# Masked global rows transposed on TensorE instead of by DMA, in a fused attention and SwiGLU kernel

## The chip, the cores and the metric

The kernel runs on one core of a Trainium2 chip. The metric is device time in microseconds for one execution, as the median of several runs. TensorE (PE) multiplies, VectorE (DVE), ScalarE (ACT) and GpSimd (POOL) do elementwise work, SyncE (SP) only issues DMAs here. Each engine works through its own queue in order.

## The reference

Eight batches of eight heads, 576 positions, head size 64. A query attends to the keys within 32 positions of it and to 8 global positions; the 8 global positions themselves attend to every key. The attention output then goes through a SwiGLU block of width 512 and inner width 1536.

```python
scores = scale * np.matmul(q, k.transpose(0, 1, 3, 2))
mask = np.abs(pos[:, None] - pos[None, :]) <= 32
mask = mask | is_global[:, None] | is_global[None, :]
attn = softmax(np.where(mask, scores, -1e9))        # over keys
x = np.matmul(attn, v).transpose(0, 2, 1, 3).reshape(4608, 512)
g = x @ w_gate
out = (g * sigmoid(g) * (x @ w_val)) @ w_out
```

Input and output are float32; the kernel multiplies in bfloat16.

## The kernel before

**FFN.** The 4608 tokens are worked in 9 chunks of 512. A chunk has 16 units (function `ffn`): 12 gate units (`gate`, L806: four matmuls for `pg` and four for `pv`, then ScalarE's tanh at L837 and VectorE's two products at L839 and L843) and 4 output units (`outp`, L867: twelve matmuls, ScalarE's copy at L872, SyncE's store at L874). The units use four one-bank PSUM buffers (tag "f"), so a unit can start when the unit two before it has been read out.

**Attention.** It is cut into steps, and each step is put by hand into the gap behind a unit of the FFN. Batch b's steps lie in chunk b-1 (gap 0 of batch b is behind unit 16(b-1); a gap of -1 is behind the last unit of the chunk before). Batch 0 runs ahead of everything, and batch 1 in chunk 0. For batch b from 2 on:

- `cast_qk` (L110, POOL) casts q and k to bfloat16 copies in DRAM; `transpose_qk` (L117, L121, SyncE) brings them back transposed as kT and qT. `load_v` (L103, POOL) loads the values va, and `load_vb` (L130, L131, SyncE) makes a copy vb that is shifted by 64 positions.
- `gather` (L252, POOL, once per two batches) fetches the rows of k and q at the global positions, kg and qg, 128 rows each, which hold 8 heads and 8 positions of both batches. `gather_mask` (L262, POOL) multiplies them with a 0/1 mask that puts each row into its place for one batch. The result is kqm: part 0 from k, part 1 from q.
- `step_GT` transposes both parts to gT. Before the change, batches 0 and 1 do it on TensorE and copy from PSUM on VectorE (L424, L429), and batches 2 to 7 by one DMA transpose on SyncE (L418).
- `step_S2` (L457) multiplies gT's part 1 with kT: the scores of the global queries against all keys. ScalarE exponentiates (L464) and VectorE masks with a table (L469), giving p2.
- `step_SG` (L435) multiplies part 0 with qT: the scores of all queries against the global keys. Exponential at L442, mask at L447, giving pg.
- `step_P2T` transposes p2 to p2t: on TensorE, with a ScalarE copy (L482, L486), for batches below XP, otherwise by a DMA on SyncE (L478).
- `step_AV2` (L492) uses p2t and va; `step_S` (L523) makes the band scores; `step_AV` (L601, L610) and `step_AV8` (L629, L637) multiply with the values and are normalised on VectorE (L577 to L583); `step_X` and `step_X8` transpose the result into xT, from batch 2 on by DMAs on SyncE (L648, L689).

A chunk c needs xT for tokens 512c to 512c+511, so chunk 2 needs the first three xT tiles of batch 2.

**Masks and parity.** In the rows of a gather, the two batches of a pair alternate in groups of 16. After the transposition the columns of an odd batch therefore stand in the other half of each group of 32 than those of an even one. Before the change each parity has its own tables: pg is masked with `mg` or, in odd batches, `mt`; p2 with `mg2` or `mg2o`. `mg2o` is made by POOL in `tables_odd` (L349 to L354) out of `cnt`, a ScalarE copy (L345) of a PSUM tile, and is put ahead of batch 1's loads in `loads_b`.

**Order.** Nothing is reordered: each engine's queue has the order in which the program calls the steps. PSUM has a pool "m" with one two-bank buffer, which step_SG, step_AV and the TensorE transposes share, and "sc" with one, for step_S2, step_S and step_AV8. The gaps of batches from 3 on, before:

```python
-1: [L(step_GT)],
1: [vb],
2: [L(step_S2), L(step_SG)] + ([L(step_P2T)] if b >= XP else []),
4: [L(step_S, 0)] + ([] if b >= XP else [L(step_P2T)]),
7: [L(step_S, 1), L(step_AV2)],
```

Of the kernel before, what the change touches and what calls it, by code (L numbers as in the profile page):

```python
# [9 lines left out]
FP32 = mybir.dt.float32  # L10
BF16 = mybir.dt.bfloat16
# [3 lines left out]
ALU = mybir.AluOpType  # L15
AX = mybir.AxisListType

P = 128
# [8 lines left out]
def kernel(  # L27
# [11 lines left out]
    nc = tc.nc  # L39

    B, H, S, D = q.shape
# [3 lines left out]
    WIN = 32  # L45
# [4 lines left out]
    HP = H // 2  # L50
    LP = 96
    LJ = S // LP
    KC = S + 2 * WIN
    XQ = 2
    XG = 2
    XB = 2
    XP = 3
    W = D + 2

    assert (B, H, S, D, NG, DM, DF) == (8, 8, 576, 64, 8, 512, 1536)  # L60
# [2 lines left out]
    const = ctx.enter_context(tc.tile_pool(name="const", bufs=1))  # L63
# [4 lines left out]
    gw = ctx.enter_context(tc.tile_pool(name="gw", bufs=2))  # L68
# [89 lines left out]
    iq = const.tile([P, KC], FP32)  # L158
# [12 lines left out]
    mt = const.tile([P, KC], BF16)  # L171
# [6 lines left out]
    def va_clear(i, eng=nc.vector):  # L178
# [8 lines left out]
        out=oh16.rearrange("p h a r -> p (h a r)"),  # L187
        in_=ident.rearrange("p (a g) -> p a g", g=NG), axis=AX.X, op=ALU.add,
# [3 lines left out]
        out=p8, in_=ident.rearrange("p (a g) -> p g a", g=NG), axis=AX.X, op=ALU.add  # L192
# [9 lines left out]
        out=mka, in_=oh16.rearrange("p h a r -> p a r h"), axis=AX.X, op=ALU.add  # L202
    )
    asel = const.tile([P, 2], FP32)
# [4 lines left out]
        out=hb, in0=bc(asel[:, 1:2], [[-1, 2]]), scalar1=float(H * S), scalar2=None, op0=ALU.mult  # L209
    )  # L210
    nc.vector.tensor_tensor(
        out=bofs_f, in0=bofs_f, in1=bc(hb, [[1, 2], [0, B // 2]]), op=ALU.add
# [4 lines left out]
        out=tmp8h, in0=dmask.rearrange("p h r -> p (h r)"), in1=i8_f, op=ALU.mult  # L217
# [4 lines left out]
        out=gidx_f, in_=gidx_i64.bitcast(I32).rearrange("p (a b) -> p a b", b=2)[:, :, 0]  # L222
# [8 lines left out]
        out=hrow, in0=hrow, scalar1=float(S), scalar2=gcol, op0=ALU.mult, op1=ALU.add  # L231
# [3 lines left out]
    thr = const.tile([P, 2], FP32)  # L235
    nc.vector.tensor_scalar(
        out=thr, in0=asel, scalar1=R2 + 0.25, scalar2=-0.25, op0=ALU.mult, op1=ALU.add
# [2 lines left out]
    nc.vector.tensor_scalar(  # L240
        out=sgn, in0=asel, scalar1=2.0, scalar2=-1.0, op0=ALU.mult, op1=ALU.add
    )
    thi = const.tile([P, 2], FP32)
    nc.vector.tensor_scalar(
        out=thi, in0=asel, scalar1=1e6, scalar2=0.5, op0=ALU.mult, op1=ALU.add
    )

    def gather(i):
# [35 lines left out]
    load_wgv(0)  # L284
    load_wgv(1)
    def loads_b():
        tables_odd()
        kT_clear(1, nc.gpsimd)
        va_clear(1, nc.gpsimd)
        gather_mask(1, *g0)  # L290
        loaded[1] = new_qk()
        load_qk_part(1, loaded[1], 0)
        load_qk_part(1, loaded[1], 1)
        load_wgv(2)
        load_v(1)
        for i in range(4):
            nc.gpsimd.dma_start(
                out=wo_sb[:, 3 * i : 3 * i + 3, :],
                in_=moe_w_out[3 * P * i : 3 * P * (i + 1), :].rearrange(
                    "(fc p) m -> p fc m", p=P  # L300
                ),
            )


    mg = const.tile([P, KC], BF16)
    mg2 = const.tile([P, KC], BF16)
    mg2o = const.tile([P, KC], BF16)
    cnt = const.tile([P, KC], BF16)

    m1 = const.tile([P, KC], BF16)  # L310

# [8 lines left out]
    def tables_a():  # L320
        nc.vector.tensor_scalar(out=band, in0=bsq, scalar1=R2, scalar2=None, op0=ALU.is_lt)
        nc.vector.tensor_scalar(
            out=mt[:, WIN : WIN + S], in0=iq[:, WIN : WIN + S], scalar1=sgn[:, 1:2],
            scalar2=thr[:, 1:2], op0=ALU.mult, op1=ALU.is_gt,
        )
        nc.vector.memset(ones, 1.0)
        kT_clear(0)
        nc.vector.tensor_scalar(
            out=mg[:, WIN : WIN + S], in0=iq[:, WIN : WIN + S], scalar1=sgn[:, 0:1], scalar2=thr[:, 0:1],
            op0=ALU.mult, op1=ALU.is_gt,  # L330
        )

    def tables_b():
        ps_i = pm.tile([P, 2, 512], FP32, tag="m", name="ps_i")
        for i in range(2):
            nc.tensor.matmul(
                out=ps_i[:, i, 0:320], lhsT=ones, rhs=m1[:, 320 * i : 320 * (i + 1)],
                start=True, stop=True,
            )
        nc.vector.scalar_tensor_tensor(  # L340
            out=mg2.rearrange("p (i c) -> p i c", i=2), in0=ps_i[:, :, 0:320], scalar=thi[:, 0:1],
            in1=mt.rearrange("p (i c) -> p i c", i=2), op0=ALU.is_lt, op1=ALU.mult,
        )

        nc.scalar.copy(out=cnt.rearrange("p (i c) -> p i c", i=2), in_=ps_i[:, :, 0:320])  # L345

    def tables_odd():

        nc.gpsimd.memset(mg[:, 0:WIN], 0.0)  # L349
        nc.gpsimd.memset(mg[:, WIN + S : KC], 0.0)  # L350
        nc.gpsimd.tensor_scalar(
            out=mg2o, in0=cnt, scalar1=thi[:, 1:2], scalar2=None, op0=ALU.is_lt
        )
        nc.gpsimd.tensor_tensor(out=mg2o, in0=mg2o, in1=mg, op=ALU.mult)  # L354

    def warm(*widths):
        ps = pf.tile([P, CH], FP32, tag="f", name="ps_w")
# [5 lines left out]
    def attention(b):  # L363
# [49 lines left out]

        def step_GT():
            kqm = kqms[b]
            if b >= XG:
                st["gT"] = gw.tile([P, 2, P], BF16, tag="gT", name="gT")
                nc.sync.dma_start_transpose(  # L418
                    out=st["gT"], in_=kqm.rearrange("p a r d -> p (a r d)")
                )  # L420
                return
            ps = mtile([P, 2, P], BF16, "ps_g")
            for a in range(2):
                nc.tensor.transpose(  # L424
                    out=ps[:, a, :], in_=kqm[:, a].rearrange("p r d -> p (r d)"),
                    identity=ident,
                )
            st["gT"] = gw.tile([P, 2, P], BF16, tag="gT", name="gT")
            nc.vector.tensor_copy(out=st["gT"], in_=ps)  # L429

        def step_SG():
            ps = pm.tile([P, 2, 512], FP32, tag="m", name="ps_sg")
            for i in range(2):
                for hp in range(HP):
                    nc.tensor.matmul(  # L435
                        out=ps[32 * hp : 32 * hp + 32, i, 0:288],
                        lhsT=st["gT"][:, 0, 32 * hp : 32 * hp + 32],
                        rhs=qTs[b][:, hp, 288 * i : 288 * (i + 1)],
                        start=True, stop=True, skip_group_check=True,
                    )  # L440
            pe = work.tile([P, S], BF16, tag="pge", name="pge")
            nc.scalar.activation(  # L442
                out=pe.rearrange("p (i c) -> p i c", i=2), in_=ps[:, :, 0:288],
                func=AF.Exp, scale=SCALE,
            )
            st["pg"] = bp.tile([P, S], BF16, tag="pg", name="pg")
            mult = lambda: nc.vector.tensor_tensor(out=st["pg"], in0=pe, in1=(mt if b % 2 else mg)[:, WIN : WIN + S], op=ALU.mult)  # L447
            if b == 0:
                st["pg*"] = mult
            else:  # L450
                mult()

        def step_S2():
            ps = psc.tile([P, 2, 512], FP32, tag="sc", name="ps_s2")
            for i in range(2):
                for hp in range(HP):
                    nc.tensor.matmul(  # L457
                        out=ps[32 * hp : 32 * hp + 32, i, 0:320],
                        lhsT=st["gT"][:, 1, 32 * hp : 32 * hp + 32],
                        rhs=kT[:, hp, 320 * i : 320 * (i + 1)],  # L460
                        start=True, stop=True, skip_group_check=True,
                    )
            pe = work.tile([P, KC], BF16, tag="p2e", name="p2e")
            nc.scalar.activation(  # L464
                out=pe.rearrange("p (i c) -> p i c", i=2), in_=ps[:, :, 0:320],
                func=AF.Exp, scale=SCALE,
            )
            st["p2"] = work.tile([P, KC], BF16, tag="p2", name="p2")
            mult = lambda: nc.vector.tensor_tensor(out=st["p2"], in0=pe, in1=mg2o if b % 2 else mg2, op=ALU.mult)  # L469
            if b == 0:  # L470
                st["p2*"] = mult
            else:
                mult()
# [291 lines left out]
            }  # L765
        if b == 2:
            return {
                0: [L(step_GT)],
                1: [vb],
                2: [L(step_S2), L(step_SG)],  # L770
                3: [L(step_S, 0), L(step_P2T)],
                5: [L(step_S, 1), L(step_AV2)],
                7: [L(step_S, 2), L(step_AV, 0), L(step_X, 0)],
                9: [L(step_S, 3), L(step_AV, 1), L(step_X, 1)],
                11: [L(step_S, 4), L(step_AV, 2), L(step_X, 2)],
                12: [L(step_AV, 3), L(step_AV8), L(step_X, 3), L(step_X8)],
            }
        return {
            -1: [L(step_GT)],
            1: [vb],  # L780
            2: [L(step_S2), L(step_SG)] + ([L(step_P2T)] if b >= XP else []),
            4: [L(step_S, 0)] + ([] if b >= XP else [L(step_P2T)]),
            7: [L(step_S, 1), L(step_AV2)],
# [190 lines left out]
```

## Time and profile before

| | us |
|---|---|
| runs shown | 381.18, 381.73, 383.14; median 381.73 |
| profiled execution | 381.18 |
| its span, first to last instruction | 379.4 |
| mean granted TensorE clock in it | 0.978 |
| TensorE matmul busy | 349.1 (92%) |
| VectorE busy | 230.3 (61%) |
| ScalarE busy | 152.0 (40%) |
| POOL busy | 96.2 (25%) |
| gT by DMA: issue to landing, shortest, median, longest of 6 | 2.3, 5.8, 8.0 |

A profile row names the engine, the line in the code, the operation and "out<-in". "Idle before" is the time that the engine stood still ahead of an instruction, and the name behind "<-" is what ended it. PE is TensorE's matmul, PEld its weight loads, SPq the queue of SyncE, which only issues. Two rows cut the span into 40 slices of 9.5 us: PEclk gives the granted clock of TensorE in tenths, DMA the busy share of the DMA engines.

### The profile page before, as it was taken

Reading aid. Unit: us, or ns where it says so; the run is one execution under the profiler, and the core shown is the slowest. Engines: PE = TensorE matmul, PEld = TensorE weight load, DVE = VectorE, ACT = ScalarE, POOL = GpSimd, SP = SyncE. Lnnn points to the kernel's source line nnn. Section 1 sums busy time; section 2 is a strip of 40 time slices with the busy share of each in tenths; the row PEclk is TensorE's granted clock in tenths of the full one; section 3 lists DMA queues with packets and bytes.
Section 4 is the critical chain, followed back from the end, with each engine's and each line's share of the span. In section 5 each row is a group of like instructions: output and inputs, shape, how many; then the busy total and the mean of one; then the engine's idle time right before and its main releaser. Section 6 shows DMA issues by size and latency. Waiting matters only on the chain.

```text
span 379.4 us, 7641 instructions
## 1 busy us (share of the span) xinstructions
PE 349.1 (92%) x3088; PEld 168.0 (44%) x3138; DVE 230.3 (61%) x460; ACT 152.0 (40%) x235; POOL 96.2 (25%) x114
## 2 busy tenths in 40 slices
PE   7899989769996999659997999999989999999996
PEld 3465445324443444224443444444434444444444
DVE  6768782528815893428735793689358935833750
ACT  5955744235323442225413452444244423323322
POOL 8896755523181012400147012000000000000000
PEclk9999999969999999969998999999999999999999
DMA  8999999999999938995499959880350051002002
GB/s 114 145 187 194 186 199 163 174 219 158 146 163 226 174 37 138 134 162 111 44 152 162 165 81 124 153 143 16 111 114 19 14 112 50 2 28 83 3 0 111
DMA packets 155940, 44.70 MB, mean 118 GB/s; under 512 B 142465, under 2 KB 150401, under 8 KB 155905
## 3 DMA queue, kind: packets, MB, share of 16 engines
q0 software_dynamic: 101216, 19.14, 63.2%
q1 hardware_dynamic: 54688, 25.07, 32.2%
q8 instruction: 24, 0.39, 0.4%
q14 instruction: 12, 0.09, 0.1%
HBM read 38.02 MB, written 16.52 MB: 144 GB/s over the span
## 4 chain that ended last, share of the span: by engine, by line
PE 59%; DMA 16%; POOL 11%; issue 9%; SPq 2%; DVE 2%; ACT 0%; POOLq 0%
PE pg L806 18%; PE po L867 17%; PE pv L806 17%; DMA gT<-kqm 6%; DMA va<-in_v_dram 5%; POOL va L103 3%; DMA wv_sb<-in_moe_w_val_dram 3%; PE ps_s L523 2%; PE ps_av L610 2%; DMA kg<-in_k_dram,gofs 2%; POOL qf L110 2%; SPq L689 1%; POOL kf L110 1%; PE ps_av L601 1%; PE ps_s L457 1%
## 5 line engine op out<-in xcount | busy, mean ns | idle before, releaser
L806 PE MATMUL pg<-xT,wg_sb 128*128 128x512 bf16 x394 | 109.0, 387 | 1.6
L806 PE MATMUL pv<-xT,wv_sb 128*128 128x512 bf16 x417 | 107.9, 381 | 0.1
L839 DVE SCALAR_TENSOR_TENSOR gv<-th,pg 128x512 bf16<-128x512 bf16 x107 | 73.3, 685 | 55.6 <-ACT th L837 55.1
L837 ACT ACTIVATE th<-pg 128x512 bf16<-128x512 f32 x107 | 63.9, 598 | 85.1 <-PE pg L806 83.5
L867 PE MATMUL po<-wo_sb,h 128*128 128x512 bf16 x400 | 92.7, 380 | 0.8
L843 DVE TENSOR_TENSOR h<-gv,pv 128x512 bf16<-128x512 bf16 x107 | 73.5, 687 | 11.2
L806 PEld LDWEIGHTS <-wv_sb 128*128 128x128 bf16 x424 | 41.9, 99 | 51.4 <-issue 2.5
L103 POOL DMA_DIRECT2D va<-in_v_dram x40 | 35.1, 989 | 116.0 <-PE ps_av L610 112.5
L806 PEld LDWEIGHTS <-wg_sb 128*128 128x128 bf16 x424 | 39.0, 99 | 46.6 <-issue 4.0
L867 PEld LDWEIGHTS <-h 128*128 128x128 bf16 x420 | 39.5, 98 | 45.4
L872 ACT ACTIVATE osb<-po 128x512 f32<-128x512 f32 x35 | 20.9, 597 | 81.3 <-PE po L867 66.6
L556 ACT ACTIVATE pe<-ps_s 128x1024 bf16<-128x1024 f32 (+1 forms) x39 | 36.4, 937 | 17.0 <-PE ps_s L523 17.0
L562 DVE TENSOR_TENSOR pt<-pe,band 128x1024 bf16<-128x1024 bf16 (+1 forms) x39 | 24.8, 635 | 14.3 <-ACT pe L556 14.3
L583 DVE TENSOR_TENSOR xa<-ps_av,den 128x512 bf16<-128x512 f32 (+1 forms) x40 | 25.5, 638 | 1.6 <-DVE den L582 0.2
L577 DVE TENSOR_REDUCE den<-ps_av 128x8 f32<-128x16 f32 (+1 forms) x40 | 6.7, 167 | 27.6 <-PE ps_av L610 25.2
L457 PE MATMUL ps_s<-kT,gT 128*32 128x320 bf16 x64 | 4.5, 363 | 18.6 <-DMA gT<-kqm 18.6
L523 PEld LDWEIGHTS <-kT 64*128 64x128 bf16 x576 | 10.7, 95 | 15.7 <-issue 15.3
L110 POOL DMA_DIRECT2D qf<-in_q_dram x6 | 16.1, 2678 | 2.3 <-DMA qf<-in_q_dram 2.3
L110 POOL DMA_DIRECT2D kf<-in_k_dram x6 | 13.5, 2254 | 10.2 <-issue 10.2
L523 PE MATMUL ps_s<-qT,kT 64*128 64x64 bf16 x576 | 15.4, 191 | 0.3 <-ACT cnt L345 0.3
L610 PE MATMUL ps_av<-vb,pt 128*64 128x66 bf16 x256 | 14.2, 197 | 1.4 <-DMA vb<-va 1.4
L464 ACT ACTIVATE p2e<-ps_s 128x640 bf16<-128x640 f32 x8 | 5.6, 704 | 24.5 <-PE ps_s L457 24.5
(148 smaller groups left out, 213.1 us busy)
## 6 DMA issues: line engine op xcount, KB each, us to landing
out_dram<-osb SPq DMA_DIRECT2D x35, 256.0 KB, 2.2
vb<-va SPq DMA_DIRECT2D x14, 264.0 KB, 7.2
kf<-in_k_dram POOLq DMA_DIRECT2D x6, 576.0 KB, 13.8
qf<-in_q_dram POOLq DMA_DIRECT2D x6, 576.0 KB, 17.0
va<-in_v_dram POOLq DMA_DIRECT2D x24, 128.0 KB, 7.5
va<-in_v_dram POOLq DMA_DIRECT2D x16, 96.0 KB, 7.1
wg_sb<-in_moe_w_gate_dram POOLq DMA_DIRECT2D x3, 512.0 KB, 9.7
wv_sb<-in_moe_w_val_dram POOLq DMA_DIRECT2D x3, 512.0 KB, 11.5
```

Of the source, the lines that this page charges most:

```text
L103: nc.gpsimd.dma_start(out=va[lo:hi, u, :, 0:D], in_=vs[t0 + lo : t0 + hi])
L110: nc.gpsimd.dma_start(out=t, in_=src[b].rearrange("h s d -> s h d"))
L523: nc.tensor.matmul(out=ps[:, par, 64 * slot : 64 * slot + 64], lhsT=kT[r : r + 64, hp, 64 * t : 64 * t + P], rhs=qTs[b][r : r + 64, hp, 64 ...
L556: nc.scalar.activation(out=pe, in_=ps[:, :, 0 : 64 * ns].rearrange("p r (s c) -> p r s c", c=64), func=AF.Exp, scale=SCALE,)
L562: mult = lambda: nc.vector.tensor_tensor(out=pt.rearrange("p r s c -> p (r s) c"), in0=pe.rearrange("p r s c -> p (r s) c"), in1=bc(band, ...
L583: nc.vector.tensor_tensor(out=xa.rearrange("p (g h) d -> p g h d", g=g), in0=bc(ps, pst + [[1, D]]), in1=bc(den, [[4, g], [1, 4], [0, D]]) ...
L610: nc.tensor.matmul(out=ps[64 * e : 64 * e + 64, hg, hl, :], lhsT=pt[:, hl % 2, 4 * (hl // 2) + 2 * (tp % 2) + e, :], rhs=(va if e == 0 els ...
L806: nc.tensor.matmul(out=ps[:, 0:n], lhsT=w[:, cc, P * fc : P * (fc + 1)], rhs=xT[:, cc, t0 : t0 + n], start=(cc == 0), stop=(cc == NCC - 1),)
L837: nc.scalar.activation(out=th[:, 0:n], in_=pg[:, 0:n], func=AF.Tanh, scale=0.5)
L839: nc.vector.scalar_tensor_tensor(out=gv[:, 0:n], in0=th[:, 0:n], scalar=1.0, in1=pg[:, 0:n], op0=ALU.add, op1=ALU.mult,)
L843: nc.vector.tensor_tensor(out=st["h"][:, fc, 0:n], in0=gv[:, 0:n], in1=pv[:, 0:n], op=ALU.mult)
L867: nc.tensor.matmul(out=po, lhsT=st["h"][:, fc, P * ts : P * (ts + 1)], rhs=wo_sb[:, fc, :], start=(fc == 0), stop=(fc == NFC - 1),)
```

## The change

- Batches 2 to 7 transpose kqm on TensorE, as batches 0 and 1 do: two 128x128 transposes into a PSUM tile of pool "m", then VectorE copies to gT. For odd batches (1, 3, 5, 7) VectorE copies in two strided halves that swap the groups of 16 columns.
- With the swap, odd batches use the even batches' tables: `mg` for pg and `mg2` for p2. `mg2o`, `cnt`, `tables_odd` and the second column of `thi` go, and `mg` loses its margins.
- step_GT moves from gap 0 (batch 2) or gap -1 (batches 3 to 7) to gap 1, one unit ahead of step_S2.
- XP goes from 3 to 4: batch 3's step_P2T is done on TensorE and ScalarE in gap 4 instead of by DMA in gap 2.

```diff
-    XG = 2
-    XP = 3
+    XP = 4
...
     def loads_b():
-        tables_odd()
         kT_clear(1, nc.gpsimd)
...
-        nc.scalar.copy(out=cnt.rearrange("p (i c) -> p i c", i=2), in_=ps_i[:, :, 0:320])
-
-    def tables_odd():
-
-        nc.gpsimd.memset(mg[:, 0:WIN], 0.0)
-        nc.gpsimd.memset(mg[:, WIN + S : KC], 0.0)
-        nc.gpsimd.tensor_scalar(
-            out=mg2o, in0=cnt, scalar1=thi[:, 1:2], scalar2=None, op0=ALU.is_lt
-        )
-        nc.gpsimd.tensor_tensor(out=mg2o, in0=mg2o, in1=mg, op=ALU.mult)
...
         def step_GT():
             kqm = kqms[b]
-            if b >= XG:
-                st["gT"] = gw.tile([P, 2, P], BF16, tag="gT", name="gT")
-                nc.sync.dma_start_transpose(
-                    out=st["gT"], in_=kqm.rearrange("p a r d -> p (a r d)")
-                )
-                return
             ps = mtile([P, 2, P], BF16, "ps_g")
...
             st["gT"] = gw.tile([P, 2, P], BF16, tag="gT", name="gT")
-            nc.vector.tensor_copy(out=st["gT"], in_=ps)
+            if b % 2 == 0:
+                nc.vector.tensor_copy(out=st["gT"], in_=ps)
+                return
+            cols = "p t (h a x) -> p (t h) a x"
+            dst, src = (t.rearrange(cols, h=HP, a=2) for t in (st["gT"], ps))
+            for a in range(2):
+                nc.vector.tensor_copy(out=dst[:, :, a], in_=src[:, :, 1 - a])
...
-            mult = lambda: nc.vector.tensor_tensor(out=st["pg"], in0=pe, in1=(mt if b % 2 else mg)[:, WIN : WIN + S], op=ALU.mult)
+            mult = lambda: nc.vector.tensor_tensor(out=st["pg"], in0=pe, in1=mg, op=ALU.mult)
...
-            mult = lambda: nc.vector.tensor_tensor(out=st["p2"], in0=pe, in1=mg2o if b % 2 else mg2, op=ALU.mult)
+            mult = lambda: nc.vector.tensor_tensor(out=st["p2"], in0=pe, in1=mg2, op=ALU.mult)
...
         if b == 2:
             return {
-                0: [L(step_GT)],
-                1: [vb],
+                1: [L(step_GT), vb],
...
         return {
-            -1: [L(step_GT)],
-            1: [vb],
+            1: [L(step_GT), vb],
```

More of the change, by code (lines that the diff above doesn't have):

```diff
@@ L242 @@
     )
-    thi = const.tile([P, 2], FP32)
+    thi = const.tile([P, 1], FP32)
     nc.vector.tensor_scalar(
-        out=thi, in0=asel, scalar1=1e6, scalar2=0.5, op0=ALU.mult, op1=ALU.add
+        out=thi, in0=asel[:, 0:1], scalar1=1e6, scalar2=0.5, op0=ALU.mult, op1=ALU.add
     )
@@ L302, in loads_b @@
             )
-    mg = const.tile([P, KC], BF16)
+    mg = const.tile([P, S], BF16)
     mg2 = const.tile([P, KC], BF16)
-    mg2o = const.tile([P, KC], BF16)
-    cnt = const.tile([P, KC], BF16)
     m1 = const.tile([P, KC], BF16)
@@ L328, in tables_a @@
         nc.vector.tensor_scalar(
-            out=mg[:, WIN : WIN + S], in0=iq[:, WIN : WIN + S], scalar1=sgn[:, 0:1], scalar2=thr[:, 0:1],
+            out=mg, in0=iq[:, WIN : WIN + S], scalar1=sgn[:, 0:1], scalar2=thr[:, 0:1],
             op0=ALU.mult, op1=ALU.is_gt,
@@ L340, in tables_b @@
         nc.vector.scalar_tensor_tensor(
-            out=mg2.rearrange("p (i c) -> p i c", i=2), in0=ps_i[:, :, 0:320], scalar=thi[:, 0:1],
+            out=mg2.rearrange("p (i c) -> p i c", i=2), in0=ps_i[:, :, 0:320], scalar=thi,
             in1=mt.rearrange("p (i c) -> p i c", i=2), op0=ALU.is_lt, op1=ALU.mult,
         )
-        nc.scalar.copy(out=cnt.rearrange("p (i c) -> p i c", i=2), in_=ps_i[:, :, 0:320])
-    def tables_odd():
-        nc.gpsimd.memset(mg[:, 0:WIN], 0.0)
-        nc.gpsimd.memset(mg[:, WIN + S : KC], 0.0)
-        nc.gpsimd.tensor_scalar(
-            out=mg2o, in0=cnt, scalar1=thi[:, 1:2], scalar2=None, op0=ALU.is_lt
-        )
-        nc.gpsimd.tensor_tensor(out=mg2o, in0=mg2o, in1=mg, op=ALU.mult)
     def warm(*widths):
```

## The prediction

> **What bounds the kernel now.** I read the page first (busy shares, the row of the granted clock, the chain that ended last), then who waited for whom, then the timeline around the longest wait, then a table of stretches cut at those waits.
>
> ```profile
> PE 349.1 (92%) x3088; PEld 168.0 (44%) x3138; DVE 230.3 (61%) x460; ACT 152.0 (40%) x235; POOL 96.2 (25%) x114
> ...
> PEclk9999999969999999969998999999999999999999
> DMA  8999999999999938995499959880350051002002
> ```
>
> TensorE is the bound at 92%, and the clock row has three dips: slices 8, 17 and 21 (each slice is 9.5 us). The list of waits says why TensorE isn't at 100%:
>
> ```profile
> PEld L457 <- DMA gT<-kqm: 21.5, 6, 7.3
> PE ps_s L457 <- DMA gT<-kqm: 18.6, 5, 6.8
> ```
>
> L457 is the first matmul of step_S2, gT the transposed global rows that a DMA brings. TensorE stood 18.6 us for it, five times: the timeline gives 5.92 (batch 2), 2.87 (3), 6.79 (4), 2.09 (5) and 0.94 (7); batch 6 had none. Its next idle reasons are 1.4 us each. Batch 2 in the timeline, SyncE's queue and TensorE:
>
> ```profile
> 64.11 5.28 SPq L121 DMA_TRANSPOSE qT<-qf  x1
> 69.43 2.04 SPq L874 DMA_DIRECT2D out_dram<-osb  x4
> 71.57 1.18 SPq L418 DMA_TRANSPOSE gT<-kqm  x1
> 72.97 0.47 SPq L130 DMA_DIRECT2D vb<-va  x1
> ...
> 79.45 0.72 PE L457 MATMUL ps_s<-kT,gT 128*32 128x320 bf16 x8 [5.92 <-DMA gT<-kqm]
> ```
>
> The transfer isn't large, it is late: kqm was ready at 63.5 us (POOL's rows at L262), but on the in-order SyncE queue it stood behind two big transposes and four output stores, and landed 7.8 us after its issue. The table of stretches (busy time of each engine, then granted clock, DMA share, GB/s) shows the price:
>
> ```profile
> 73.50:118.30 44.80, 38.57 (x334) 17.92 (x339) 25.23 (x50) 15.98 (x24) 16.71 (x15) 0.92 1.86 180
> 118.30:158.30 40.00, 36.71 (x328) 17.29 (x334) 25.49 (x50) 15.28 (x23) 8.71 (x7) 1.00 1.18 131
> 158.30:203.50 45.20, 38.14 (x328) 17.65 (x334) 25.36 (x50) 15.33 (x23) 10.00 (x10) 0.92 0.90 122
> 203.50:244.20 40.70, 38.29 (x329) 17.71 (x335) 25.36 (x50) 15.33 (x23) 6.59 (x10) 0.96 1.14 133
> 244.20:281.20 37.00, 36.68 (x329) 17.30 (x334) 25.35 (x50) 15.28 (x23) 0.00 (x0) 1.00 0.47 97
> ```
>
> Each stretch is one chunk of 512 tokens with one batch's attention, the same work. The undisturbed one takes 37.0 us, the others 40.0 to 45.2. The excess is the wait, and in three of them a second cost: the clock is granted at 0.50 after the wait (75.91 to 82.74, 161.25 to 168.07, 205.62 to 209.03).
>
> **What the change removes.** (1) The idle time: 18.6 us. (2) The half clock: what TensorE does from its restart to the end of the dip runs at half speed: 79.45 to 82.74, 165.04 to 168.07, 205.61 to 209.03, together 9.7 us, half of it lost: 4.9 us. (That this is proportional: step_S2 and step_SG take 1.14 us there, 79.45 to 80.59, against 0.63 at full clock, 121.20 to 121.83.) Profiled execution 381.18 - 18.6 - 4.9 = 357.7 us if nothing new comes.
>
> The dip came after 2.09 us of idleness (batch 5) but not after 2.87 us (batch 3), so here what counts is not the length alone. [...] The trace has the dip begin as the 2.09 us end, so I keep the row.
>
> (3) The early tables of the odd batches: 3.8 us of POOL (L351 2.11, L354 1.61, two memsets) and ScalarE's cast cnt, 0.69 us at 10.08. The head of the kernel ends on the loads of va (TensorE waits 0.45 us at L492 until one lands at 17.37), issued ahead of both, so the cast gives nothing: 0, at most that wait's order of size, 0.4. Freed POOL issues batch 1's loads at 21.1 in place of 24.87, but its queue still carries weights until 28.3, and no TensorE wait names them: 0, at most 0.5.
>
> **What it adds.** (a) Two TensorE transposes per batch, 2 to 7. Row: the two of L696 between two gate units move the next unit's start by 0.12 us (68.07 to 69.92 instead of 1.73 after). 6 x 0.12 = 0.7 us, all on the path. Bound above: their own 0.28 us, 1.7.
>
> [...]
>
> (b) Batch 3's transposes of p2 go from a DMA to TensorE (XP 3 to 4): five after step_S(0), as batch 2 has them at 83.81: start of scores to next unit 0.63 against 0.34 without: 0.3 us. ScalarE copies 0.69 more, at 40% busy: 0.
>
> (c) VectorE copies gT: 0.29 us for even batches (L429), two strided halves for odd ones. The trace doesn't show the halves: one is at least 0.15 (L504, 128x4), at most 0.29; I take 0.2, nearer the small one as each has half the elements. VectorE's queue: the copy stands behind unit 1's two products and ahead of unit 2's. In batch 2 these end at 73.10, TensorE is free for step_S2 at 73.5, so an even copy ends about in time; batch 3: 117.89 plus 0.4 to 0.6 against 118.3. I take 0.1 per even and 0.2 per odd batch: 0.9 us. Below it is 0; above, a copy behind one more product (0.69) is about 1.0 each, 6. Behind the copy waits unit 2's product, 0.3 to 0.5 late; it is wanted two units (3.5 us) later. Batch 1's copy also becomes two halves: hidden, 0 to 0.3.
>
> (d) What is late next, batch 2: qT. It was issued at 64.11 and landed 10.9 us later:
>
> ```profile
> DMA to landing us min/median/max: 10.9/10.9/10.9
> ```
>
> That is 75.0; step_SG would want it at about 73.7. 1.3 us stay; 0.5 to 2.
>
> (e) xT of batch 2. From here TensorE is 6 us earlier, the DMAs are not: their row shows 9 to slice 13. Unit 32 starts chunk 2 at 112.8 and needs the third xT tile, issued 103.8, landed 7.0 us later at 110.8 (2.4 us in quiet stretches). Now it is wanted at 106.6 and can be issued at 97.6, behind qT of batch 3, which landed at 101.0. Three tiles at 1.3 us after that give 105 to 108: I take 0.5, from 0 to 3, and a dip of 1.7 at the upper end.
>
> (f) p2t, batches 4 to 7, now issued soon after vb in place of 8 us later. Batch 5's landed 7.9 us after issue, 10 us after step_S2; step_AV2 comes 10 us after step_S2. 0.5, from 0 to 2. vb itself has seven units until step_AV(0), and its slowest landing was 8.5 us: 0.
>
> SyncE loses six gT issues of 1.2 us and one p2t; vb moves up by as much. kqm is ready long before gap 1 (63.5, 116.4 and 206 us), so the transposes find it there.
>
> Sum: 357.7 + 0.7 + 0.3 + 0.9 + 1.3 + 0.5 + 0.5 = **361.9 us**, against the profiled execution's 381.18. That one is the lowest of the three; their median is 0.55 higher, so the forecast for a median is **362.4 us**.
>
> **Rivals.**
> *The DMAs are the bound until 133 us.* TensorE gains on gT and gives it back on xT, qT or vb of batches 2 and 3. For it: DMA 9 in every slice up to there, share 1.86 in the first stretch above, landings three times those of quiet stretches. Against: most of that traffic is early; batch 4's qT had landed at 133.8 and is wanted at 158, batch 5's casts at 126.6. The gains lost are 5.9 + 1.6 - 1.3 + 2.9 = 9.1: 371.5.
>
> *VectorE becomes the wait: slower than before.* The copy is in order behind the gate products, and VectorE is 61% busy, with slices at 9. If it ends over 2.1 us after unit 2, TensorE idles that in each of six batches, and 2.1 us was enough for a dip of 1.7: in place of (c), 6 x 3.8 = 22.8, which gives 361.9 - 0.9 + 22.8 + 0.55 = 384.4. Below 2.1 us, without dips, it stays faster (374 just under it). Against: in all six batches unit 1's products end 0.3 to 0.4 us before unit 2's matmuls do, and the undisturbed chunk ran at 37.0 us with VectorE in the same order.
>
> [...]
>
> *It doesn't take the wait away.* Only if kqm were late; it isn't.
>
> **Numbers.** Forecast 0.77 (358.5 to 366); dips stay 0.08; DMA-bound 0.11; slower 0.03; something in the noise 0.01. Low end: no cost but (a) and (b), 358.7. High end: (a) 1.7, (c) 3, (d) 2, (e) 3, (f) 1 is 368.4. I give 358.5 to 368. What a measurement can tell from no change is about 0.5%, 1.9 us. Faster 0.96, same 0.01, slower 0.03.
>
> **What will show it.** Right: no wait at step_S2's line above 1 us but batch 2's on qT; the stretches near 37.5 us; mean clock 0.99 or more instead of 0.978; TensorE near 97%. Wrong: TensorE waiting at unit 32 or at step_AV2; a gT copy starting after unit 2's first product; dips at new places.

## The result and the profile after

The changed kernel took **358.51 us** (median of 4 runs, 357.63 to 360.10) against 381.46 (4 runs, 380.26 to 383.14): a ratio of 0.940, 95% interval 0.9351 to 0.9449. The forecast was 362.4, so the direction and the mechanism held, and the measured time lies at the very low end of the range. The profiled execution took 358.50, its span is 356.7, and the mean granted clock is 1.000 instead of 0.978. The ratios and intervals in this document leave out executions that took over 1.5% longer than the fastest of the same kernel; the medians keep them.

The page of the changed kernel, the same three rows as before the change:

```profile
PE 345.5 (97%) x3105; PEld 167.6 (47%) x3155; DVE 231.7 (65%) x470; ACT 151.9 (43%) x235; POOL 93.0 (26%) x110
...
PEclk9999999999999999999999999999999999999999
DMA  7999999999999999997899979613520230011002
```

TensorE's busy share rose from 92% to 97%, and no slice of the clock row dips. The two lines on gT by DMA are gone from the list of waits. What TensorE or its weight loads wait for at the places in question is now:

```profile
PEld L420 <- DMA qT<-qf: 2.0, 1, 2.0
PE ps_sg L420 <- DMA qT<-qf: 1.7, 1, 1.7
PEld L442 <- DVE gT L409: 1.6, 4, 0.4
...
PEld L442 <- DVE gT L414: 1.3, 3, 0.4
```

L442 is step_S2 (L457 before). Its weight loads run ahead of the matmuls and meet VectorE's copies (L409 even, L414 odd) 0.4 us early; the matmuls themselves then start without a gap in batches 3 to 7. The one wait left is the third line of the timeline of batch 2:

```profile
71.15 0.28 DVE L409 COPY gT<-ps_g 128x256 bf16<-128x256 bf16 x1
...
71.72 0.46 PE L442 MATMUL ps_s<-kT,gT 128*32 128x320 bf16 x8
...
73.86 0.43 PE L420 MATMUL ps_sg<-qT,gT 128*32 128x288 bf16 x8 [1.68 <-DMA qT<-qf]
```

step_S2 starts at once; step_SG stands 1.68 us for qT. The table of stretches, cut at step_S2 of batches 2 to 7 (length, busy PE, PEld, DVE, ACT, POOL, granted clock, DMA share, GB/s):

```profile
71.70:111.00 39.30, 37.21 (x340) 17.64 (x349) 25.44 (x52) 16.09 (x24) 10.61 (x9) 1.00 1.80 184
111.00:148.40 37.40, 36.93 (x339) 17.71 (x349) 25.61 (x51) 15.83 (x24) 14.80 (x13) 1.00 1.73 158
148.40:185.40 37.00, 36.68 (x330) 17.33 (x336) 25.50 (x52) 15.29 (x23) 10.03 (x10) 1.00 1.14 151
185.40:222.50 37.10, 36.78 (x331) 17.41 (x336) 25.73 (x51) 15.29 (x23) 7.01 (x10) 1.00 1.32 145
222.50:259.60 37.10, 36.78 (x333) 17.43 (x339) 25.60 (x52) 15.28 (x23) 0.00 (x0) 1.00 0.44 96
```

The last three stretches run at the 37.0 us of the undisturbed chunk. The first (39.3) holds the wait for qT, the second (37.4) batch 3's transposes of p2.

### The profile page after: what moved, and what is told of

Its sections match the earlier page's. It is cut to its first block, busy times and chain, and to the rows that moved or that the text cites. A ratio compares the mean times of both kernels' runs of the same rounds, so it can differ in the third digit from the quotient of the medians.

```text
span 356.7 us, 7667 instructions
## 1 busy us (share of the span) xinstructions
PE 345.5 (97%) x3105; PEld 167.6 (47%) x3155; DVE 231.7 (65%) x470; ACT 151.9 (43%) x235; POOL 93.0 (26%) x110
## 4 chain that ended last, share of the span: by engine, by line
PE 81%; DMA 11%; POOL 5%; issue 1%; DVE 0%; ACT 0%; POOLq 0%
PE po L850 25%; PE pg L789 23%; PE pv L789 23%; DMA qT<-qf 3%; DMA k_bf<-in_k_dram 3%; PE ps_av L595 3%; DMA va<-in_v_dram 3%; PE ps_s L508 3%; DMA vb<-va 2%; POOL va L102 1%; PE ps_av L586 1%; PE po L837 1%; PE ps_av L477 1%; PE ps_s L442 1%; PE ps_sg L420 0%
## 5 line engine op out<-in xcount | busy, mean ns | idle before, releaser
L789 PE MATMUL pg<-xT,wg_sb 128*128 128x512 bf16 x398 | 106.5, 380 | 1.6 <-issue 0.2
L789 PE MATMUL pv<-xT,wv_sb 128*128 128x512 bf16 x413 | 106.6, 379 | 0.2
L595 PE MATMUL ps_av<-va,pt 128*64 128x66 bf16 x256 | 14.4, 197 | 0.0
L595 PEld LDWEIGHTS <-pt 128*64 128x64 bf16 x512 | 10.8, 110 | 4.7 <-DMA vb<-va 0.6
```

What stands on the lines that cost most here:

```text
L595: nc.tensor.matmul(out=ps[64 * e : 64 * e + 64, hg, hl, :], lhsT=pt[:, hl % 2, 4 * (hl // 2) + 2 * (tp % 2) + e, :], rhs=(va if e == 0 els ...
L789: nc.tensor.matmul(out=ps[:, 0:n], lhsT=w[:, cc, P * fc : P * (fc + 1)], rhs=xT[:, cc, t0 : t0 + n], start=(cc == 0), stop=(cc == NCC - 1),)
```

## The experiments

My theory: the gain is the wait for gT and the half clock behind it, because gT stood late in SyncE's queue. Rivals: a good part comes from the early tables; a DMA transpose is slow wherever it stands; the clock dips have another cause; VectorE's copy is free anyway. Times of the kernel before beside these runs: 383.93 us (experiments 1 to 4), 381.69 (5 to 8) and 384.09 (9 to 12), with single runs from 377.0 to 386.4.

**Experiments 1 to 3: the early tables.** The removed early work is put back, unused: both parts, ScalarE's alone, POOL's alone.

```diff
+        nc.scalar.copy(out=cnt..., in_=ps_i[:, :, 0:320])         # 1 and 2
...
     def loads_b():
+        nc.gpsimd.tensor_scalar(out=mg2o, in0=cnt, ...)            # 1; in0=m1 in 3
+        nc.gpsimd.tensor_tensor(out=mg2o, in0=mg2o, in1=mt, ...)   # 1 and 3
```

> The changed kernel with the removed early work put back, its results unused: ScalarE's cast cnt and POOL's two operations on mg2o ahead of batch 1's loads (POOL reads mt where it read mg; the two small memsets stay out). Theory (the early tables held up batch 1's loads and so vb, 1.9 us by the traces): 360.4 us. Rival (my prediction: the weights in the DMA queue hide it, 0): 358.5 us, and TensorE's wait for vb in batch 1 stays at 0.5 us.

> The changed kernel with ScalarE's cast cnt alone put back, result unused. Theory (the head's 0.6 to 0.9 us are lost again at the load of wv and at vb, so the cast alone is worth little): 358.5 to 359.0 us. Rival (the cast is most of the early gain): 360 us.

> The changed kernel with POOL's 3.7 us of table work alone put back ahead of batch 1's loads, result unused (it reads m1 where it read cnt). Theory (POOL's share is what holds up the DMA stream): 359.5 to 360 us, TensorE's wait for vb in batch 1 back at 1.4 us. Rival (hidden behind the weights' transfers): 358.5 us.

Measured: 358.77 us (ratio 0.9452, 0.9418 to 0.9487), 358.86 (0.9452, 0.9416 to 0.9487) and 358.69 (0.945, 0.9413 to 0.9486). None is apart from the changed kernel (358.51, and 359.52 when it was run again), though that one was not run beside them. The three were run side by side, and they settle it: experiment 1 has POOL's work and experiment 2 hasn't, experiment 1 has the cast and experiment 3 hasn't, and all agree within 0.2 us. TensorE even waited for the cast again (0.50 us in experiment 1, 0.82 in 2), and the time didn't grow; its wait for vb was 0.57, 0.63 and 0.41 us, not 1.4. My theory of the moment, 1.9 us, which I had read from one pair of traces, falls; the 0 of the prediction holds. One pair of landings suggests why. The third part of wg is issued on POOL at 23.03 us in the changed kernel, and at 26.51 with POOL's work back. The first line below is its time to landing in the changed kernel, the second with POOL's work back:

```profile
DMA to landing us min/median/max: 13.3/13.3/13.3
```

```profile
DMA to landing us min/median/max: 10.2/10.2/10.2
```

They land within 0.4 us of each other, at 36.3 and 36.7: issued 3.5 us earlier, the transfer took 3.1 us longer. That the transfers ahead of it held it up would explain this; it isn't shown.

**Experiments 4 and 10: step_SG of batch 2 one gap later**, run twice, the second time beside the changed kernel (experiment 9).

```diff
-                2: [L(step_S2), L(step_SG)],
-                3: [L(step_S, 0), L(step_P2T)],
+                2: [L(step_S2)],
+                3: [L(step_SG), L(step_S, 0)],
+                4: [L(step_P2T)],
```

> The changed kernel with batch 2's step_SG one gap later (gap 3) and its step_P2T in gap 4, so that a gate unit of 1.73 us stands between step_S2 and the first use of qT. Theory (qT is the last wait above 0.5 us on the path): 356.8 us and no TensorE wait over 0.5 us. Rival (DMAs bound this stretch, the wait moves to vb or xT of batch 2): 358.5 us with a new wait of 1 to 2 us.

> The changed kernel once more, on the chip of the next three, as what they are compared with: 358.5 us.

> Batch 2's step_SG and step_P2T one gap later, as before, now beside the changed kernel itself. Theory (a gate unit fills the wait for qT, 0 to 1.9 us by execution): 0.5 to 1.5 us under the changed kernel. Rival (the wait moves elsewhere): no difference.

Measured: 358.03 us (0.943, 0.9394 to 0.9465); then 358.02 (0.9362, 0.931 to 0.9415) beside 359.52 for the changed kernel (0.9387, 0.9335 to 0.9438). In both traces TensorE has no wait for qT in batch 2 left, as the theory says; the time didn't reach the 356.8 us that it named. Beside the changed kernel the median is 1.5 us lower, but the intervals overlap: likely, not shown. In the trace of experiment 4 another wait stood out, for vb in batch 1:

```profile
PE ps_av L595 <- DMA vb<-va: 2.8, 1, 2.8
```

That line's wait is 0.5 us in the changed kernel's trace, and in experiment 10, with the same edit, 0.3 us, so the early waits differ between executions of the same code.

**Experiment 5: gT still by DMA, but earlier in the queue** (the kernel before).

```diff
-                0: [L(step_GT)],                    # batch 2
+                -3: [L(step_GT)],
...
-            -1: [L(step_GT)],                       # batches 3 to 7
+            -2 if b % 2 == 0 else -8: [L(step_GT)],
```

> The kernel before, gT still by DMA, with step_GT moved earlier in SyncE's queue: gap -3 for batch 2, -8 for odd batches from 3, -2 for batches 4 and 6. Theory (the transfer was late, not slow): the waits of batches 3 to 7 go with their dips (2.9 + 8.2 + 3.8 + 0.9 = 15.8) and batch 2's shrinks to about 1.5 us without a dip (6): 360 us. Rival (a DMA transpose costs its 6 to 8 us wherever it stands): 375 us or more.

Measured: 369.33 us, ratio 0.9645 (0.956 to 0.9731): 10 us above the changed kernel, between the two theories. Of the list of waits in the trace, from 60 us on:

```profile
PE ps_s L457 <- DMA gT<-kqm: 8.1, 2, 4.3
```

Two waits are left of five, 3.77 us in batch 2 and 4.29 in batch 4, each with a dip of the clock. Batches 3, 5, 6 and 7 don't wait. Batch 3's gT, issued at 96.28, still took 6.5 us to land, but 13 us ahead of its use. Batch 2's, issued at 70.32 behind two output stores, took 6.9, and batch 4's 6.0:

```profile
148.31 2.44 SPq L689 DMA_TRANSPOSE xT<-xa  x2
151.25 1.18 SPq L418 DMA_TRANSPOSE gT<-kqm  x1
```

It still stood behind batch 3's xT, because the program makes kqm of batch 4 behind unit 45 (its gap -3), and the transfer has to come behind that. So the transfer is both: late, and slower in batches 2 to 4 (6.0 to 6.9 us) than in batches 5 to 7 (2.3 to 2.6). In the kernel before, the six landings took 7.8, 6.9, 8.0, 4.7, 2.3 and 2.3 us, with a DMA share of 1.95, 1.98, 2.05, 1.00, 0.45 and 0.45 between issue and landing. Moving it by seven gaps (batches 3, 5 and 7) ended the waits; by three (batch 2) or one (batch 4) it only shortened them, from 5.92 to 3.77 and from 6.79 to 4.29 us. For batch 4 that limit is the program's, not the data's. POOL ran ahead and had made its rows by 117.6 us, 34 us before the transfer was issued:

```profile
117.20 0.39 POOL L262 TENSOR_TENSOR kqm<-qg,mka 128x128 bf16<-128x128 f32 x1
```

A version that also moves the mask step, and with it the transfer, further ahead was not run. So it is open how near to the changed kernel a DMA placed early enough would come.

**Experiment 6: the waits filled with matmuls** (the kernel before).

```diff
-                2: [L(step_S2), L(step_SG)],                                # batch 2
+                2: [L(warm, *[512] * 26), L(step_S2), L(step_SG)],
...
-            2: [L(step_S2), L(step_SG)] + ([...
+            2: [L(warm, *[512] * {4: 30, 5: 9}.get(b, 0)), L(step_S2), L(step_SG)] + ([...
```

> The kernel before, with 26, 30 and 9 matmuls of 512 columns, results unused, put ahead of step_S2 of batches 2, 4 and 5, which fill the waits of 5.9, 6.8 and 2.1 us and use no new data. Theory (the half-clock stretches come from TensorE's idleness): the waits end when they did, the dips go, 4.9 us less: 376.6 us, mean clock near 1.0. Rival (the dips have another cause): 381.5 us or more, clock 0.978.

Measured: 379.95 us (10 runs, 378.0 to 383.8) against 381.69, ratio 1.0007 (0.9949 to 1.0065): no difference shown. The profiled execution took 378.10 and has no dip. Its clock row, and what is left of the waits:

```profile
PEclk9999999999999999999999999999999999999999
```

```profile
PE ps_s L459 <- DMA gT<-kqm: 6.4, 4, 2.1
```

In this execution the dips went with the idleness: with the waits of batches 2, 4 and 5 filled its mean clock is 1.000, against 0.978 in the profiled execution of the kernel before. The other nine executions had mean clocks of 0.991 to 1.000, against 0.969 to 0.986 for the kernel before beside them. Most of them still had a dip or two, by my estimate: 3.41 us at a clock of 0.50 take 0.0045 off the mean over 376 us. That the dips cost 4.9 us by themselves isn't shown. Behind the filled wait of batch 5 TensorE still stood 1.69 us, and in batch 6 it now stood 1.58 where it had not before. With the full clock TensorE reaches the next gT earlier, and if gT doesn't come as much earlier, part of the gain goes into that wait. Between the two profiled executions 3.1 us of the half clock's 4.9 show up, but single runs of either kernel scatter by more than that.

**Experiment 7: step_GT right ahead of step_S2.**

```diff
-            1: [L(step_GT), vb],
-            2: [L(step_S2), L(step_SG)] + ([...
+            1: [vb],
+            2: [L(step_GT), L(step_S2), L(step_SG)] + ([...
```

> The changed kernel with step_GT in gap 2, right ahead of step_S2, for batches 2 to 7, so that VectorE's copy of gT stands behind unit 2's two products. Theory (the gate unit between step_GT and step_S2 is what hides the copy): TensorE waits 1.6 to 1.9 us in each of six batches, 10 us: 368.5 us, no dips. Rival (VectorE's copy costs nothing wherever it stands): 358.5 us. Third: waits over 2 us bring dips: 375 us or more.

Measured: 367.55 us, ratio 0.9615 (0.9537 to 0.9693), as the theory said. The timeline of batch 7:

```profile
266.30 0.28 PE L403 MATMUL ps_g<-ident,kqm 128*128 128x128 bf16 x2
267.05 0.69 DVE L826 TENSOR_TENSOR h<-gv,pv 128x512 bf16<-128x512 bf16 x1
267.66 0.35 DVE L414 COPY gT<-ps_g 128x128 bf16<-128x128 bf16 x2
268.06 0.46 PE L442 MATMUL ps_s<-kT,gT 128*32 128x320 bf16 x8 [1.49 <-DVE gT L414]
```

The copy takes 0.35 us, the wait is 1.49: most of it is the gate product ahead of the copy in VectorE's queue. The six waits are 1.43 (even) and 1.49 (odd), 8.8 us together, and none brought a dip: the mean granted clock is 1.000, and the eight matmuls of step_S2 took 0.46 us in all six batches, as at full clock, against 0.72 at half clock before. In the changed kernel the same copies stand one unit earlier and cost nothing:

```profile
258.42 0.69 DVE L826 TENSOR_TENSOR h<-gv,pv 128x512 bf16<-128x512 bf16 x1
258.64 1.03 PE L789 MATMUL pv<-xT,wv_sb 128*128 128x512 bf16 x4
259.03 0.35 DVE L414 COPY gT<-ps_g 128x128 bf16<-128x128 bf16 x2
259.59 0.46 PE L442 MATMUL ps_s<-kT,gT 128*32 128x320 bf16 x8
```

**Experiment 8: batch 3's p2 by DMA again.**

```diff
-    XP = 4
+    XP = 3
```

> The changed kernel with XP back at 3, batch 3's p2 transposed by a DMA. Theory (five transposes on TensorE cost 0.3 us and nothing waits for the DMA): 358.2 us. Rival (its p2t lands late, in the stretch where the DMAs are full): 359 us or more and a TensorE wait at step_AV2 of batch 3.

Measured: 359.56 us, ratio 0.94 (0.9326 to 0.9474). In time it isn't apart from the changed kernel; its profiled execution had a wait of 2.0 us for wv at 22.7 us, with a dip, that has nothing to do with the edit. The trace decides for the theory: the stretch of batch 3 is 0.3 us shorter than the 37.40 above, and nothing waits at step_AV2.

```profile
112.10:149.20 37.10, 36.62 (x330) 17.41 (x336) 25.53 (x51) 15.28 (x23) 14.74 (x13) 1.00 1.89 163
```

**Experiments 11 and 12: batch 1's vb by POOL**, alone and with experiment 10's edit.

```diff
-                st["vb"] = load_vb(0)
+                st["vb"] = bp.tile([P, 4, H, W], BF16, tag="vb", name="vb")
...
-                2: [L(step_GT), L(step_T, 2)], 3: [L(step_T, 3), vb],       # batch 1
+                2: [L(step_GT), L(step_T, 2)],
+                3: [L(step_T, 3)] + [L(shift, t, nc.gpsimd.tensor_copy) for t in range(4)],
```

> The changed kernel with batch 1's vb made by eight POOL copies instead of two DMAs (batch 0's way, 0.65 us each), behind the issue of batch 2's casts. Theory (those two DMAs compete with the casts, and TensorE waits for them 0.4 to 2.8 us by execution): no TensorE wait for vb in batch 1, 0.5 to 1 us under the changed kernel. Rival (POOL's loads of va for batch 2 come 5 us later, and TensorE or the copies themselves wait): same or slower by 1 to 3 us.

> Both edits, step_SG later and vb by POOL. Theory: the head gives TensorE no wait over 0.5 us before the last batch, 356 to 357.5 us. Rival (one of the two costs what the other gains): 358.5 us.

Measured: 358.21 us (0.9356, 0.9305 to 0.9406) and 358.13 (0.9361, 0.931 to 0.9412), beside 359.52. No wait for vb is left in either trace; in experiment 11 TensorE waits 0.67 us for VectorE (gvt) at the same place instead. Experiments 10, 11 and 12 all lie 1.3 to 1.5 us under the changed kernel by the median, and the two edits together give no more than one; the 356 to 357.5 us expected of both weren't reached. All intervals against the kernel before overlap. Run by run, five of the changed kernel's six times here (358.2 to 359.8) lie above all six of experiment 11 (357.3 to 358.7), so a gain of about 1 us is likely; a version that beats the changed kernel for certain isn't shown.

## Why the prediction was right, and where its sizes were off

The mechanism held, and every sign that the prediction named for it came: no wait at step_S2's line above 1 us, 1.68 us for qT of batch 2, stretches of 37.0 to 37.4 us behind the first, clock 1.000, TensorE at 97%. That the median lies inside the range is luck. The range begins at 358.5 and the median is 358.51; run again (experiment 9), the same kernel took 359.52. The ends were also worked out loosely: 358.7 and 368.4 are sums for the profiled execution, without the 0.55 us added for a median, and the high end leaves out (b) and takes 3 and 1 us for (c) and (f), whose own bounds were 6 and 2.

**(1) and (2), idle time and half clock: 23.5 us, held as a sum.** Both are gone, and the pace of the last chunks (37.0 to 37.1 us) is the one that the undisturbed chunk had. How the gain divides between the two isn't shown (experiment 6).

**(3), early tables: 0, held** (experiments 1 to 3). The two profiled executions differ by 1.86 us at the first output unit (54.39 and 52.53), but that is scatter between executions, not the tables: in experiment 9, the changed kernel again, the unit began at 54.41.

**(a), TensorE transposes: 0.7, held.** In the timeline of the changed kernel the unit behind a pair starts 0.11 us later: 1.84 us after the one before it (68.06), against 1.73.

```profile
69.79 0.28 PE L403 MATMUL ps_g<-ident,kqm 128*128 128x128 bf16 x2
69.90 1.03 PE L789 MATMUL pg<-xT,wg_sb 128*128 128x512 bf16 x4
```

**(b): 0.3, held** (experiment 8).

**(c), VectorE's copies: 0.9 forecast, 0 measured.** Apart from qT's landing, this is the largest miss. The halves take 0.215 us each, near the 0.2 assumed. But I let the copy's end run into step_S2's start; in the rows of the changed kernel the odd copy ends at 259.38 and the matmuls start at 259.59, where they would have started anyway. The hiding is real and narrow: experiment 7 moves the same copy by one unit and pays 1.46 us each time.

**(d), qT of batch 2: 1.3 forecast, 1.68 in the profile, and the term is better put as a fixed time.** step_SG of batch 2 starts within 0.06 us of qT's landing in the traces of the changed kernel and of experiments 1, 2, 3, 8 and 9 (73.86 after 73.81; 74.91, 74.97, 73.47, 75.01 and 74.72 after 74.87, 74.93, 73.43, 74.97 and 74.67). So an earlier head only waits longer there: 1.68 us in the changed kernel, 0.66 in experiment 9; in experiments 3 and 8 TensorE arrived just as qT landed. What follows is constant: span minus that start is 282.8, 282.8 and 282.9 us in the changed kernel and experiments 3 and 9. The prediction took 75.0 from one execution; the landing ranges from 73.4 to 75.0. That is 1.2 us of the miss, and it is scatter: with a landing at 74.67, experiment 9's profiled execution took 359.51 us.

**(e), xT of batch 2 at unit 32: 0.5 forecast, 0 measured, but close.** The third tile was issued at 96.57, took 8.3 us, landed at 104.9, and unit 32 began at 105.6. **(f), p2t: 0.5 forecast, 0 measured**: the landings took 2.6 to 7.8 us and no step_AV2 waited for one.

The sum: 361.9 forecast, 358.5 measured in the profiled executions; 1.9 of the 3.4 are (c), (e) and (f), 1.2 is qT's landing, and 0.3 stays open. The 0.55 us added for a median was a property of the kernel before; the changed kernel's median and profiled execution agree within 0.01.

**The rivals.** *The DMAs bound it until 133 us* didn't come true, but the wait for qT of batch 2 is of that kind, and (e) stayed clear of one by only 0.7 us. *VectorE becomes the wait* needed 2.1 us; experiment 7 shows that even without the gate unit it is 1.5 and without dips, so the kernel stays faster than before. *Dips stay* (chance 0.08): no dip in the changed kernel's profile, one of 3.41 us in those of experiments 1 and 2 (behind qT), 4 (vb) and 8 (wv).

## What to carry to other kernels

A small transfer that gates the bound engine should be priced by what stands ahead of it in its queue and by how full the DMAs are, not by its size: here six transfers of 64 KB cost 18.6 us of waiting, and the same transfer landed 2.3 us after its issue at a DMA share of 0.45 and 8.0 us after it at 2.05. Moving it to the bound engine cost 0.11 us per batch, but only because one unit of other work stood between the transposes and their use, so that the copy behind them was hidden. And when the first stall of a chain goes, ask which landing comes next and put it into the sum as a time on the clock: here TensorE gained nothing by arriving earlier at qT, with 282.8 us left from there after a wait of 1.68 us and 282.9 after one of 0.66.

## What the runs showed of the hardware

**The half-clock stretches had two lengths.** Every one that began behind a wait lasted 3.41 or 6.83 us. In the kernel before, the full clock between them lasted 78.51 us (82.74 to 161.25) and 37.55 us (168.07 to 205.62), 23 and 11 times 3.41. Idle times of 1.84 us (experiment 1), 1.94 (2), 2.0 (8), 2.09 (kernel before, batch 5) and 2.8 (4) were followed by one; 1.68 (changed kernel), 2.10 (experiment 6, batch 3) and 2.87 (kernel before, batch 3) weren't. Experiment 1's, in the table of stretches, with the granted clock of 0.50:

```profile
75.72:79.13 3.41, 3.41 (x25) 1.36 (x24) 1.77 (x3) 1.00 (x3) 0.00 (x0) 0.50 1.23 323
```

So the puzzle of the prediction, a dip behind 2.09 us and none behind 2.87, stays open: the length of the wait alone didn't decide it, and no run shows what did. The 2.1 us that the prediction took as enough for a dip is one row of one execution: 1.84 us was enough in experiment 1, and 2.10 wasn't in experiment 6.

**In experiment 11 POOL's copies and VectorE's products took longer side by side.** The first band product of 128x1024 beside POOL's copies of vb took 1.01 us and the second 1.07, against 0.68 to 0.72 at the same places in the changed kernel. The third took 0.69, and there POOL's copy took 1.18 us instead of 0.62. That they slow each other would explain this; it isn't shown.

```profile
46.24 0.62 POOL L698 COPY vb<-va 64x528 bf16<-64x528 bf16 x1
...
46.39 1.01 DVE L547 TENSOR_TENSOR pt<-pe,band 128x1024 bf16<-128x1024 bf16 x1 [0.69 <-ACT pe L541]
...
51.69 1.18 POOL L699 COPY vb<-va 64x528 bf16<-64x528 bf16 x1
51.70 0.69 DVE L547 TENSOR_TENSOR pt<-pe,band 128x1024 bf16<-128x1024 bf16 x1
```
